# A local-attention and channel-mixing kernel on one core: the whole table that orders its steps is replaced

## The chip, the cores and the metric

The kernel runs on one core of a Trainium2 chip. The metric is the time of one execution on the device in microseconds (us); lower is better. Before the change three runs gave 621.28, 622.59 and 622.96 us, median 622.59 us.

## What is computed

The reference, cut to what matters (4 batches, 8 heads, 768 positions, 64 values a head):

```python
k_sum = k.reshape(B, H, nb, 32, D).max(axis=3)          # block maxima, 24 blocks
v_sum = v.reshape(B, H, nb, 32, D).mean(axis=3)         # block means
scores_l = scale * q @ k^T   where |i - j| < 16, else -1e9
scores_s = scale * q @ k_sum^T + log(32)
a = softmax(concat(scores_l, scores_s))                 # local window and block summaries
x = (a @ concat(v, v_sum)) laid out as [batch, 768, 512]
u = x + (x^T @ U @ V)^T                                 # U, V of rank 32, over the positions
out = u + relu(u @ w_ch1) @ w_ch2                       # 512 -> 2048 -> 512
```

## The kernel before the change

Everything is held in two parts (a high one and a rest) so that the products keep 32-bit accuracy; a product is therefore three matmuls. The bulk of the work is TensorE's (PE): for batch 0 the rows of `up` (L1015) and `down_rows` (L1037), for batches 1 to 3 the seven products of `up_phase` (L1300, inside `product`) and then `down_phase` (L1396) or, in batch 3, `second_phase` (L1498). All else is small steps round it: each batch's attention is done while PE works on the batch before it, and the weights are scaled, summed, stored to memory, fetched again and split as they are needed.

The order in which these steps are issued is a table of words, the string `PLAN` (L67 on). It has 481 pieces between slashes. After each piece of PE's main work the kernel runs the words of the next piece:

```python
def go():
    for word in next(plan).split():
        name = word.rstrip("0123456789.")
        words_of[name](*map(int, filter(None, word[len(name) :].split("."))))
```

The schedule is manual: every engine carries out its instructions in the order in which the words issue them, so a word's place fixes its place on PE, on the vector engine (DVE), the scalar engine (ACT), GpSimd (POOL) and on the queue of SyncE (SP), which issues all transfers one after the other. A transfer's issue waits on SP until its source is written, and everything behind it waits with it.

The first piece, up to the first slash, is the start-up: batch 0's attention (words with a leading dot), before PE's main work can begin. Its words load k, q and v of a head (`.lk`, `.lq`, `.lv`; L310, L324, L345), reduce block maxima (`.K`, L418), make scores (`.S`, L474), exponentials (`.E`), transposes, block means of v by a matmul (`.M`, L399), the value summaries (`.B`, `.D`, L437), values (`.V`, L599), the division by the sum (`.N`, L629), the mixing over positions (`.I`, L642, and what follows), and now and then four matmuls on zeros (`.w4`, L1139).

For a head h of batches 1 to 3 (written b.h) the words are, in the order of its data: scores `S` (PE L451), exponentials `E` (DVE L499, ACT L509), `T` (the weights are transposed in 32x32 squares, DVE L529), `s` (the squares go to memory, SP L534), `f` (four transfers bring them back transposed, SP L542), `P` (the values, PE L613) and `N` (the division, DVE L627 to L629, which writes `x`). The squares have one buffer. Then, for a pair of heads, `M` mixes over the positions (PE L642). For two of the four channel groups `x` is also transposed on the way through memory: `R` (DVE L554), `r` (SP L558, `rows<-place`), `g` (four transfers, SP L567, `place<-rows`), after which L692 on PE and L695 on DVE add the mixing to the rows. Other words met below are `w` (sums of weights, DVE L874 to L878), `y` (the low part of a gate, DVE L1374, 1.78 us in a row below), `O` (the operands of the seven products, among them DVE L743 and L757), `F` (a weight fetched, SP L929), `G` (parts of the down weights stored, SP L990, `halfA<-parts`), `Us`, `U` and `D` (SP L894, L883 to L885, L890), `v` (SP L338 and L339).

Of the kernel before, what the change touches and what calls it, by code (L numbers as in the profile page):

```python
# [73 lines left out]
    .S6 .Xl .C4 .la0 .S4 .K5 .Qs .E14.0 .Bd2 .Dp1 .E8.1 .V5 .E13.0 l1.0.0 .Kp5 .V4 .E8.2 .N0 .S5
    .E12.2 .E8.0 .V3 .V2 .E11.1 .E13.1 .E12.0 .M1 .lr .E9.0 .E12.1 .E11.2 .T12 .E13.2 .E11.0
    .E9.1 .T8 .T15 .Mo1 .Z0 .C12 .C15 .Dp6 .E10.2 .E10.1 .la1 .Qf .E10.0 .N1 .N2 .T13 .lb0 .T14
    .I0 .Y0.0 .T11 .E9.2 .Bd6 .Dd5 .T9 .Io0 .C11 .Bp4 .Bp7 .C13 .la2 .C8 .Y0.1 .Dp4 .V12 .lb1
    .C9 .V11 .V13 .Y0.2 .J0 .lb2 .V8 .N6 .la4 .Bp5 .T10 a1.0.0 .la3 .V9 .C14 .V14 .Jo0 .C10 q1.0
    .V10 .Dp7 .N4 k1.0 .G0.0 .V15 .G0.1 .lb3 .N5 .Z1 .N7 .Go0.0 a1.0.0 .G1.1 .Go0.1 .I2 .G1.0
    .Y1.0 .Io2 .J2 .z0 .w4 .Y1.1 .Jo2 .G0.2 .W0 .G0.3 .Y1.2 .Go0.2 l1.0.1 .Go0.3 .Z2 .G1.2  # L80
    .Go1.1 .Go1.2 a1.0.0 t2 W0.5 .G1.3 a1.0.0 .Go1.0 t2 .Go1.3 .U0.0 .W1 a1.0.0 / / / t2 c0.4 t2
    t2 a1.0.0 K1.0 .lb4 t2 c0.3 t3 a1.0.0 a1.0.1 w0.0 c1.2 / l1.1.0 w0.1 / x1.1 t3 x0.2 t3 v1.1
    D1 Ka1.0 v1.0 / c1.3 k1.1 S1.0.1 / E1.0.1.0 E1.0.1.1 W0.6 E1.0.1.2 S1.0.0 t3 a1.0.1 t4
    E1.0.0.1 t3 c0.5 E1.0.0.0 D0 K1.1 t5 a1.0.1 E1.0.0.2 a1.0.1 t3 Ka1.1 x0.3 w1.0 / T1.0 x1.2
    q1.1 k1.2 K1.2 / / c1.4 S1.1.0 a1.0.1 t4 / E1.1.0.2 W1.5 U0 S1.1.1 E1.1.0.0 a1.1.0 E1.1.0.1
    W1.6 s1.0 Ka1.2 q1.2 U1 w1.1 E1.1.1.2 E1.1.1.0 t4 a1.0.1 D2 E1.1.1.1 t4 k1.3 Us0 t4 t4 t5 t5
    Us1 f1.0 / c1.5 U4 a1.0.1 a1.0.1 x1.3 / D3 x0.4 a1.0.1 c0.6 / W0.7 t6 S1.2.0 t5 Ba1.1.1 U3
    T1.1 W0.8 E1.2.0.1 Ba1.0.0 E1.2.0.0 a1.1.0 E1.2.0.2 / t5 s1.1 t5 / q1.3 x0.5 W1.7 t6 x1.4
    a1.1.0 D4 S1.2.1 W0.9 Ba1.0.1 E1.2.1.1 K1.3 f1.1 E1.2.1.2 / E1.2.1.0 t6 / t6 c0.7 c0.8 P1.0
    Ba1.1.0 t6 / c1.6 W1.8 N1.0 T1.2 w2.0 t7 Ka1.3 t8 k1.4 / S1.3.0 / s1.2 E1.3.0.2 E1.3.0.0  # L90
    S1.3.1 t6 E1.3.0.1 q1.4 c1.7 P1.1 w2.1 k1.5 x1.5 E1.3.1.0 E1.3.1.1 t7 v1.2 E1.3.1.2 N1.1
    K1.4 x0.6 t7 T1.3 Ka1.4 / Ba1.2.1 / t7 v1.3 c1.8 q1.5 t7 w3.0 t7 / S1.4.0 Ba1.2.0 x1.6 U5
    f1.2 D5 E1.4.0.2 W1.9 R1.0 c0.9 t8 K1.5 x0.7 E1.4.0.0 w3.1 l1.1.1 t8 / Ba1.3.1 W0.10 / /
    E1.4.0.1 W0.11 S1.4.1 Ba1.3.0 E1.4.1.0 E1.4.1.2 E1.4.1.1 a1.1.0 t8 P1.2 t9 s1.3 t9 N1.2 t8
    t8 / / x1.7 T1.4 W1.10 x0.8 q1.6 Ka1.5 c0.10 U6 / a1.1.1 S1.5.0 t10 / f1.3 a1.1.0 E1.5.0.2
    S1.5.1 D7 W1.11 D6 E1.5.0.1 c1.9 t9 t10 E1.5.0.0 t9 t9 c0.11 k1.6 a1.1.1 E1.5.1.1 c1.11 t10
    U7 t11 t9 r1.0 / s1.4 a1.1.0 W0.12 E1.5.1.0 a1.1.1 t10 x1.8 / a1.1.0 g1.0 a1.1.1 E1.5.1.2
# [1567 lines left out]
```

## Time and profile before

| what | us |
|---|---|
| median of three runs (621.28 to 622.96) | 622.59 |
| the profiled execution's own time | 626.52 |
| its span, from the first to the last instruction | 624.3 |
| first matmul of the main work | 50.25 |
| busy: PE, weight loads of PE | 610.4, 557.9 |
| busy: DVE, ACT, POOL | 446.5, 350.9, 345.6 |

The profile shows one execution. "PE" is the matmuls and "PEld" PE's loading of the stationary operand, which overlaps them. A matmul's busy time ends where the profile models its end, so two matmuls in a row overlap in the record. Each row of an engine gives the time that the engine sat idle before it and, after an arrow, what ended that idleness. The chain of waits is followed back from the last instruction: each piece is an engine or a transfer on which the next piece waited.

### The profile page before, as it was taken

How to read it: one execution, taken by the hardware profiler on the slowest of the kernel's cores; microseconds unless marked ns; L12 is line 12 of the kernel's file. 1: busy time of each engine (PE TensorE's matmuls, PEld its weight loads, DVE VectorE, ACT ScalarE, POOL GpSimd, SP SyncE). 2: the span in 40 equal slices, each digit the busy share in tenths (PEclk: the TensorE clock that was granted, in tenths of full speed). 3: DMA queues.
4: the chain of work that ended last, by engine and by line, in shares of the span. 5: the costliest groups of instructions: out<-in, count | busy, mean ns of one | idle time of the engine just before them, and what ended most of it. 6: DMA issues, size and time to landing. Idle time of an engine off the chain costs nothing.

```text
span 624.3 us, 14694 instructions
## 1 busy us (share of the span) xinstructions
PE 610.4 (98%) x5376; PEld 557.9 (89%) x5376; DVE 446.5 (72%) x1139; ACT 350.9 (56%) x794; POOL 345.6 (55%) x393
## 2 busy tenths in 40 slices
...
GB/s 222 230 323 246 285 313 258 288 291 325 295 197 281 226 239 262 241 301 300 262 305 181 210 266 203 198 256 237 253 242 311 220 133 168 149 191 203 145 119 126
DMA packets 97559, 148.30 MB, mean 238 GB/s; under 512 B 9680, under 2 KB 67920, under 8 KB 97488
## 3 DMA queue, kind: packets, MB, share of 16 engines
...
q14 instruction: 29, 0.24, 0.1%
...
## 4 chain that ended last, share of the span: by engine, by line
PE 81%; DMA 12%; SPq 3%; DVE 1%; issue 1%; ACT 1%; POOL 1%; DVEq 0%; ACTq 0%
PE ps_h L1300 25%; PE acc L1396 17%; PE ps_h L1015 10%; PE acc L1037 10%; PE accx L1498 4%; PE accy L1498 3%; PE accz L1498 3%; DMA place<-in_k 2%; PE ps_x L613 2%; DMA dsum<-tmp 2%; PE ps_s L474 2%; PE ps_s L451 2%; DMA there<-squares 2%; SPq L542 1%; DMA whole<-up 1%; DMA place<-in_v 1%
## 5 line engine op out<-in xcount | busy, mean ns | idle before, releaser
L967 POOL TENSOR_TENSOR parts<-whole,parts 128x512 fp32r<-128x512 f32 (+1 forms) x128 | 159.3, 1258 | 77.3 <-ACT parts L963 72.9
L1300 PE MATMUL ps_h<-place,parts 128*128 128x384 f32 x1008 | 179.5, 336 | 0.7 <-DVE x L629 0.7
L1300 PEld LDWEIGHTS ps_h<-place,parts 128*128 128x128 f32 x1008 | 174.3, 188 | 3.0 <-PE ps_h L1300 1.0
L1396 PE MATMUL acc<-gh,parts 128*128 128x256 f32 (+1 forms) x512 | 133.6, 341 | 0.0
L1396 PEld LDWEIGHTS acc<-gh,parts 128*128 128x128 f32 x512 | 88.6, 189 | 12.3 <-issue 1.4
L963 ACT CAST parts<-whole 128x512 fp32r<-128x512 f32 (+1 forms) x144 | 80.8, 581 | 11.9 <-issue 4.6
L1396 PE MATMUL acc<-gl,parts 128*128 128x512 f32 (+1 forms) x256 | 86.5, 338 | 0.0
L1015 PE MATMUL ps_h<-place 128*128 128x384 f32 x384 | 73.9, 341 | 0.4 <-DVE x L695 0.3
L509 ACT ACTIVATE e<-e,neg 128x120 f32<-128x120 f32 x144 | 52.0, 390 | 33.4 <-DVE neg L499 32.3
L1015 PEld LDWEIGHTS ps_h<-place 128*128 128x128 f32 x384 | 67.2, 188 | 3.1 <-DVE x L695 0.7
L1037 PE MATMUL acc<-place,gh 128*128 128x512 f32 x192 | 66.5, 400 | 0.0
L1369 ACT ACTIVATE gh<-place 128x768 fp32r<-128x768 f32 x32 | 27.1, 846 | 62.2 <-PE acc L1396 62.2
L264 POOL TENSOR_SCALAR val<-place 128x512 f32<-128x512 f32 (+1 forms) x33 | 54.1, 1642 | 9.4 <-ACT place L244 4.4
L289 POOL TENSOR_TENSOR place<-val,place 128x512 fp32r<-128x512 f32 x29 | 37.6, 1301 | 29.7 <-ACT place L288 25.2
L1374 DVE SCALAR_TENSOR_TENSOR gl<-place,gh 128x768 fp32r<-128x768 f32 x32 | 38.3, 1196 | 20.3 <-ACT gh L1369 20.2
L1396 PEld LDWEIGHTS acc<-gl,parts 128*128 128x128 f32 x256 | 48.5, 189 | 4.5 <-DVE gl L1374 0.2
L743 POOL TENSOR_TENSOR place<-tmp,place 128x384 fp32r<-128x384 f32 x24 | 27.8, 1163 | 41.0 <-ACT place L739 34.2
L1037 PEld LDWEIGHTS acc<-place,gh 128*128 128x128 f32 x192 | 36.1, 188 | 7.4 <-ACT gh L1027 0.2
L499 DVE CUSTOM_DVE_ANT_0 e<-ps_s,mask_sb 128x120 f32<-128x120 f32 x144 | 35.1, 276 | 6.2 <-PE ps_s L451 4.1
L1027 ACT ACTIVATE gh<-ps_h 128x384 fp32r<-128x384 f32 x32 | 15.7, 489 | 41.0 <-PE ps_h L1015 40.9
L1037 PE MATMUL acc<-place,gl 128*128 128x512 f32 x96 | 37.7, 393 | 0.0
L1329 DVE TENSOR_TENSOR place<-place,ps_h 128x384 f32<-128x384 f32 x24 | 13.3, 554 | 28.7 <-PE ps_h L1300 28.6
...
## 6 DMA issues: line engine op xcount, KB each, us to landing
...
there<-squares SPq DMA_DIRECT2D x24, 384.0 KB, 4.8
at<-there SPq DMA_DIRECT2D x96, 96.0 KB, 3.4
whole<-up SPq DMA_DIRECT2D x24, 384.0 KB, 3.9
...
```

Source lines behind the costliest of these rows:

```text
L264: nc.gpsimd.tensor_scalar(f32(bits), f32(hi), 0.0, None, ALU.mult)
L289: engine.tensor_tensor(lo, val, f32(hi), ALU.subtract)
L499: nc.vector.tensor_tensor_reduce(out=e[:, u, :], in0=ps[:, i * KC : (i + 1) * KC], in1=mask_sb[:, m, :], scale=-SCALE, scalar=BIG, op0=ALU ...
L509: nc.scalar.activation(e[:, u, :], e[:, u, :], AF.Exp, bias=st.neg[h][:, u : u + 1], scale=-1.0,)
L963: nc.scalar.copy(hi, whole)
L967: (nc.vector if key[0] == "second" else nc.gpsimd).tensor_tensor(lo, whole, f32(hi), ALU.subtract)
L1015: nc.tensor.matmul(ps[:, :NH], w_split[0, f][:, c % 2, part_w, c // 2], ut[c], start=(n == 0), stop=(n == 3 * NC - 1),)
L1037: nc.tensor.matmul(acc[t], gt[:, sl], w_split[1, f][:, part_w], start=(first and j == 0), stop=(last and j == 2),)
L1300: nc.tensor.matmul(ps, a[:, sa, i], b[i][:, sb], start=(first and n == 0), stop=(n == 5), skip_group_check=not first,)
L1374: nc.vector.scalar_tensor_tensor(gl, h, 0.0, f32(gh), ALU.max, ALU.subtract)
L1396: nc.tensor.matmul(place, w[:, part_w, c * P : (c + 1) * P], gt[:, q0:q1], start=(f == 0 and i == 0 and j == 0), stop=(f == NF - 1 and j = ...
L1498: nc.tensor.matmul(ps, w[j][:, sa, c * P : (c + 1) * P], gate[sb], start=fresh and q == 0 and j == 0 and k == 0, stop=q == 3 and j == 1 an ...
```

## The change

The string `PLAN` is replaced by another with the same words: 1882 words in 481 pieces, each as often as before. No other line differs; what the words do is untouched. Nearly every line of the table differs, so two lines of each stand for it:

```diff
 PLAN = """
-    .lu .li .X .w4 .z1 .w4 .lk0 .lk3 .K0 .Xt0 .Kd0 .lq0 .lm .lq3 .lk2 .K3 .S0 .Kd3 .S3 .m .K2
-    .Kp2 .E0.2 .w4 .lq2 .E0.1 .lk1 .F .w4 .lq1 .E1.0 .E7.0 .E6.2 .E1.1 .lv0 .S2 .lv1 .E0.0 .E1.2
...
+    .lu .lq2 .lk0 .K0 .lk2 .lq0 .w4 .X .w4 .Kd0 .w4 .lq3 .K2 .lk3 .lm .S0 .Kp2 .K3 .S2 .Kd3 .m
+    .lk1 .S3 .E4.1 .E7.0 .li .K1 .E5.0 .E5.2 .E1.0 .E5.1 .lq1 .E1.2 .lv0 .E6.1 .E7.2 .lv1 .Xt0
...
```

Three places where the order of instructions moves follow, each as the lists of the two kernels have it: the line of the code, the operation, output and input tiles with their buffer numbers, and the shape.

**SP's queue where batch 1 sends the rows of its channel groups 2 and 3 through memory.** Before, the second `rows` transfer (`rows_2888`, word r1.3) stands behind the four fetches of the first (`place_2881`, word g1.2):

```order
L929 DMA whole_2763<-up0_104 128x1024
L558 DMA rows_2810<-place_2723 128x768
L894 DMA up5_109<-place_2218 128x512
L894 DMA up5_109<-place_2219 128x512
L929 DMA whole_2861<-up0_104 128x768
L567 DMA place_2881<-rows_2810 32x4x192 x4
L558 DMA rows_2888<-place_2830 128x768
L310 DMA kt_2890<-in_k 128x3x192
L929 DMA whole_2892<-up1_105 128x1024
L567 DMA place_2903<-rows_2888 32x4x192 x4
```

With the change the first `rows` transfer is `rows_2728`, the second `rows_2860`:

```order
L558 DMA rows_2728<-place_2643 128x768
L542 DMA at_2752<-there_2678 32x4x192 x4
L929 DMA whole_2759<-up0_104 128x1024
L894 DMA up5_109<-place_2209 128x512
L894 DMA up5_109<-place_2210 128x512
L890 DMA down_112<-val_2260 128x512
L567 DMA place_2831<-rows_2728 32x4x192 x4
L890 DMA down_112<-val_2631 128x512
L558 DMA rows_2860<-place_2836 128x768
L324 DMA qz0_84<-in_q0 64x384
L324 DMA qz0_84<-in_q1 64x384
L567 DMA place_2895<-rows_2860 32x4x192 x4
```

The first `rows` transfer has moved ahead of a head's fetch (L542, the last of batch 1) and stands further from its own fetches; a k load and a weight fetch no longer stand between the second `rows` transfer and its fetches, two q loads do.

**DVE's order where batch 2's last two heads are divided by their sums** (words N2.6 and N2.7: L627 to L629, the tiles `sum`). Before, both divisions follow one another behind an operand step and a gate (`gl_4821`):

```order
L984 TENSOR_TENSOR tmp_4813<-whole_4590,tmp_4806 128x256
L985 TENSOR_TENSOR tmp_4813<-whole_4590 128x256
L743 TENSOR_TENSOR place_4619<-x_3716,place_4619 128x384
L757 TENSOR_TENSOR tmp_4874<-x_3716 128x384
L1374 SCALAR_TENSOR_TENSOR gl_4821<-place_3772,gh_4820 128x768
L627 TENSOR_SCALAR sum_4888<-ps_x_4713 128x6
L628 RECIPROCAL sum_4888<-sum_4888 128x6
L629 TENSOR_TENSOR x_3716<-ps_x_4713,sum_4888 128x6x64
L627 TENSOR_SCALAR sum_4898<-ps_x_4848 128x6
L628 RECIPROCAL sum_4898<-sum_4898 128x6
L629 TENSOR_TENSOR x_3716<-ps_x_4848,sum_4898 128x6x64
L554 STREAM_TRANSPOSE place_4903<-x_3716 128x768
```

With the change:

```order
L984 TENSOR_TENSOR tmp_4836<-whole_4641,tmp_4676 128x256
L985 TENSOR_TENSOR tmp_4836<-whole_4641 128x256
L695 TENSOR_TENSOR x_3780<-ps_u_4839,place_4582 128x3x128
L627 TENSOR_SCALAR sum_4868<-ps_x_4843 128x6
L628 RECIPROCAL sum_4868<-sum_4868 128x6
L629 TENSOR_TENSOR x_3780<-ps_x_4843,sum_4868 128x6x64
L1374 SCALAR_TENSOR_TENSOR gl_4889<-place_3770,gh_4888 128x768
L757 TENSOR_TENSOR tmp_4903<-tmp_4730,x_3780 128x384
L433 COPY kt_4595<-km_4688 64x4x12 x4
L984 TENSOR_TENSOR tmp_4921<-whole_4690,tmp_4783 128x256
L985 TENSOR_TENSOR tmp_4921<-whole_4690 128x256
L554 STREAM_TRANSPOSE place_4951<-x_3780 128x768
```

The last division (`sum_4868`) now stands ahead of the gate (`gl_4889`) and of the operand step; the one of the head before it (`sum_4779`) stands ten rows above the first row shown. The transpose L554 has five rows of other work between the division and itself.

**SP's queue where head 4 of batch 1 is fetched** (word f1.4: `at<-there`, L542). Before, the squares were sent as `there_2001` ten rows above it:

```order
L894 DMA up3_107<-place_1709 128x512
L894 DMA up3_107<-place_1710 128x512
L542 DMA at_2204<-there_2001 32x4x192 x4
L883 DMA up1_105<-val_977 128x512
L883 DMA up5_109<-val_1930 128x512
L558 DMA rows_2248<-place_2118 128x768
```

With the change the squares (`there_2159`) are sent nineteen rows above it:

```order
L338 DMA vt_2332<-in_v 96x390
L339 DMA vt_2332<-in_v 96x390
L534 DMA there_2339<-squares_2220 128x768
L883 DMA up4_108<-val_1713 128x512
L883 DMA up5_109<-val_1947 128x512
L885 DMA up5_109<-val_2074 128x2x128
L890 DMA down_112<-val_1948 128x512
L542 DMA at_2396<-there_2159 32x4x192 x4
L802 DMA place_2449<-in_w2 128x1024
```

The fetch has moved down the queue, behind the sending of head 5's squares (`there_2339`), the rows of channel group 1 and two heads' loads of v; in the table it now stands in the same piece as the values of its head (P1.4).

## Rows read from the trace of the kernel before

**Rows 1.** The page: busy time, share of the span and instructions of each engine; the group of the seven products' matmuls (busy time, mean ns of one, idle time before them).

```profile
PE 610.4 (98%) x5376; PEld 557.9 (89%) x5376; DVE 446.5 (72%) x1139; ACT 350.9 (56%) x794; POOL 345.6 (55%) x393
...
L1300 PE MATMUL ps_h<-place,parts 128*128 128x384 f32 x1008 | 179.5, 336 | 0.7 <-DVE x L629 0.7
```

**Rows 2.** The chain of waits, in order of time: start, length (us), what.

```profile
25.46 7.87 DMA place<-in_v
...
50.25 4.30 PE ps_h L1015 x24
54.55 1.62 PE acc L1037 x7
...
504.08 56.16 PE ps_h L1300 x324
```

**Rows 3.** All waits of PE in the span: line, what was waited for, us in total, times, the longest (lines left out are of the start, none over 1.0 us).

```profile
PE ps_s L474 <- DMA x<-in_q: 3.5, 2, 2.8
PE ps_n L399 <- DMA place<-in_v: 1.2, 2, 0.8
...
PE ps_m L642 <- DVE x L629: 0.8, 2, 0.6
PE ps_h L1300 <- DVE x L629: 0.7, 1, 0.7
...
PE ps_x L613 <- DMA whole<-up: 0.4, 1, 0.4
PE ps_x L613 <- DMA at<-there: 0.4, 1, 0.4
PE ps_h L1015 <- DVE x L695: 0.3, 1, 0.3
PE ps_u L692 <- DVE x L695: 0.3, 1, 0.3
...
```

**Rows 4.** SP's queue from 183 to 198 us: start, us, the issue, and how many in a row (times are those of issuing, not of the transfer).

```profile
183.77 0.38 SPq L558 DMA_DIRECT2D rows<-place  x1
...
190.22 2.47 SPq L567 DMA_DIRECT2D place<-rows  x4
192.73 0.43 SPq L558 DMA_DIRECT2D rows<-place  x1
...
195.59 1.74 SPq L567 DMA_DIRECT2D place<-rows  x4
```

**Rows 5.** The chain of waits at the same place: the transfers of the second `rows` and of its fetch.

```profile
192.73 2.85 DMA rows<-place
...
196.91 4.40 DMA place<-rows
```

**Rows 6.** DVE at the same place: start, us, line, operation, and in brackets the idle time before it and what ended it.

```profile
189.91 0.98 DVE L554 STREAM_TRANSPOSE place<-x 128x768 f32<-128x768 f32 x1
...
196.91 1.51 DVE L878 TENSOR_TENSOR place<-val,place 128x256 f32<-128x256 f32 x1
198.46 0.56 DVE L695 TENSOR_TENSOR x<-ps_u,place 128x384 f32<-128x384 f32 x1
...
201.49 0.56 DVE L695 TENSOR_TENSOR x<-ps_u,place 128x384 f32<-128x384 f32 x1 [1.55 <-DMA place<-rows]
```

**Rows 7.** DVE from 334 to 338 us, same columns.

```profile
334.49 0.56 DVE L757 TENSOR_TENSOR tmp<-x 128x384 f32<-128x384 f32 x1 [1.81 <-DMA dsum<-tmp]
334.96 1.78 DVE L1374 SCALAR_TENSOR_TENSOR gl<-place,gh 128x768 fp32r<-128x768 f32 x1
336.66 0.15 DVE L627 TENSOR_SCALAR sum<-ps_x 128x6 f32<-128x6 f32 x1
...
337.96 0.56 DVE L629 TENSOR_TENSOR x<-ps_x,sum 128x384 f32<-128x384 f32 x1
```

**Rows 8.** DVE from 266 to 269 us, same columns.

```profile
266.28 0.98 DVE L529 STREAM_TRANSPOSE squares<-e 128x768 f32<-128x768 f32 x1 [2.03 <-POOL parts L967]
...
268.71 0.56 DVE L629 TENSOR_TENSOR x<-ps_x,sum 128x384 f32<-128x384 f32 x1
```

**Rows 9.** The page's transfer issues: operation, count, size of one, median us from issue to landing.

```profile
there<-squares SPq DMA_DIRECT2D x24, 384.0 KB, 4.8
at<-there SPq DMA_DIRECT2D x96, 96.0 KB, 3.4
```

**Rows 10.** SP's queue: the sending and the fetch for head 7 of batch 3, and what stands between.

```profile
465.91 0.38 SPq L534 DMA_DIRECT2D there<-squares  x1
...
466.81 3.52 SPq L990 DMA_DIRECT2D halfA<-parts  x4
470.45 2.57 SPq L542 DMA_DIRECT2D at<-there  x4
```

**Rows 11.** SP's queue and PE: the fetch for head 4 of batch 1 and the matmuls that read it.

```profile
137.06 3.35 SPq L542 DMA_DIRECT2D at<-there  x4
...
160.04 0.89 PE L613 MATMUL ps_x<-vt,at 120*32 120x65 f32 x48
```

**Rows 12.** Stretches of the span: us, busy us of PE, PEld, DVE, ACT and POOL with the count of instructions, PE's granted clock, busy share of the transfer engines, GB/s moved.

```profile
20.00:22.00 2.00, 1.88 (x78) 1.54 (x66) 0.75 (x3) 0.87 (x4) 0.60 (x2) 1.00 0.65 166
22.00:24.00 2.00, 1.49 (x34) 1.11 (x36) 1.57 (x5) 1.92 (x6) 1.74 (x6) 1.00 0.73 194
...
500.00:550.00 50.00, 50.00 (x290) 49.55 (x289) 23.20 (x39) 32.24 (x71) 34.13 (x31) 1.00 0.46 144
```

More of the change, by code (lines that the diff above doesn't have):

```diff
@@ L74 @@
[L74 to L97, printed above, removed]
@@ new lines @@
+    .V9 .Y1.0 .N5 .N4 .Y1.1 .G0.1 .w4 .I2 .Go0.1 l1.0.1 .Io2 .G0.0 .Go0.0 .J2 .G1.0 .Jo2 .lb2
+    .G1.1 .G0.3 .G0.2 .Y1.2 .G1.3 .la3 k1.0 .la4 .W0 .G1.2 .Go0.3 .Go0.2 k1.1 .Z2 t2 .Go1.0
+    .Go1.2 .Go1.1 a1.0.0 U0 .Go1.3 .U0.0 .W1 / K1.0 a1.0.1 a1.0.0 t2 w0.0 / a1.0.0 c1.2 / t2
+    a1.0.0 t2 t2 c0.3 t2 .lb3 / a1.0.1 a1.0.0 .z0 w0.1 t3 Ka1.0 a1.0.0 / S1.0.1 t3 x1.1 x0.2 /
+    c0.4 W0.5 v1.0 t4 / S1.0.0 E1.0.1.0 c0.5 .lb4 .z1 a1.0.1 D1 l1.1.0 W0.6 E1.0.1.2 c1.3
+    E1.0.1.1 t3 q1.1 a1.1.0 t3 E1.0.0.0 t3 a1.0.1 k1.2 E1.0.0.2 K1.1 E1.0.0.1 t3 q1.2 W1.5 t5 /
@@ new lines @@
+    E1.3.0.2 s1.2 E1.3.0.1 t7 D3 W1.7 E1.3.0.0 x1.5 S1.3.1 E1.3.1.0 t7 l1.1.1 E1.3.1.2 v1.3 W0.9
+    P1.1 Ba1.2.0 Ba1.2.1 E1.3.1.1 N1.1 W1.9 t7 Ba1.3.1 c1.8 k1.5 / w2.1 W0.10 K1.4 t7 Ka1.4 t7
+    c1.7 t7 c0.9 T1.3 U2 R1.0 t8 x1.6 / / a1.1.1 S1.4.0 E1.4.0.2 f1.2 E1.4.0.0 t8 K1.5 c1.9
+    a1.1.1 W1.10 E1.4.0.1 w3.0 t8 x0.7 / / t8 t8 / w3.1 S1.4.1 t8 U7 t9 q1.5 s1.3 D5 / r1.0
+    Ba1.3.0 / E1.4.1.2 t9 P1.2 U6 E1.4.1.0 x1.7 U5 Ka1.5 E1.4.1.1 c0.10 t9 t9 / N1.2 W0.11 /
+    S1.5.0 T1.4 x0.8 t10 a1.1.1 c0.11 E1.5.0.2 a1.1.0 E1.5.0.1 f1.3 t9 k1.6 g1.0 E1.5.0.0 /
```

190 lines of the change are left out of this document (101 added, 89 removed).

## Prediction

> **What bounds the kernel now.** I read the busy times first: PE is busy for 610.4 of 624.3 us [rows 1]. A busy PE need not be a PE at its peak, so I took a stretch in which it waits for nothing. The chain of waits stays on PE for 324 matmuls from 504.08 us, 56.16 us or 173 ns each [rows 2], and in 500 to 550 us PE's loads were busy for 49.55 of 50 us at full granted clock, with DVE at 23.20 and POOL at 34.13 [rows 12]. There a matmul starts as fast as its stationary operand can be loaded, and no order of the other engines' work makes that faster. An order can win only what PE waits for: the start, up to the first matmul of the main work at 50.25 us [rows 2], and the waits after it. Those are few: 0.8, 0.7, 0.4, 0.4, 0.3 and 0.3 us, 2.9 us in seven waits [rows 3].
>
> A shown wait is smaller than its delay. A matmul's record lasts 336 ns on average [rows 1] where one starts each 173 ns, so the record covers 0.16 us of the time after the next should have begun. I count shown time plus 0.16 us for each wait: 2.9 + 7 x 0.16 = 4.0 us after 50.25 us. That is the most that the order can win there.
>
> The Trainium skill, "Perfetto Trace Analysis", section Identifying the Most-Contended Engine, judges TensorE's headroom by the busy share of weight loads, not by that of matmuls. By that rule 624.3 - 557.9 = 66 us would be open to a better order, not 4 plus the start. The rows speak against it here: loads fill 99% of the wait-free stretch at one matmul each 173 ns, but one of L1037 takes 231 ns [rows 2], so that the same load fills some 74% of it with PE just as busy. I keep to the waits.
>
> **The change, place by place.** No word is added or removed, so the engines' work is the same, and the sum has terms only for waits that go or come. The gains:
>
> *A, batch 1's rows, 199 to 202 us: -0.9.* PE waits twice, 0.3 us each, on L695 [rows 3]. The second L695 sat idle for its fetch until 201.49 [rows 6]. The transpose that makes those rows was over at 190.89 (189.91 + 0.98) [rows 6], but they were sent at 192.73, when SP had issued the four fetches of the group before (190.22 to 192.69) [rows 4]; then 2.85 us to memory and 4.40 us back [rows 5]. The first L695 started at 198.46, behind L878, which ran 1.51 us from 196.91 [rows 6]. In the new order the first group's rows are sent ahead of a fetch and stand further from their own fetches, so SP should be past these by 190.9; the 1.8 us so won cover the 1.55 us of idleness. L877 and L878 now come behind three L695. Both waits go: 0.6 + 2 x 0.16 = 0.9. Bounds: 0 and -0.9.
>
> *B, batch 2's last divisions, 337 to 339 us: -1.1.* The mixing L642 waits twice, 0.8 us in all, on L629 [rows 3]. The two divisions stood behind an L757, which waited 1.81 us for a buffer until 334.49, and a gate of 1.78 us, and ran from 336.66 to 338.52 [rows 7]. Now N2.7 stands ahead of gate and operand step, N2.6 ten rows higher, and 32 matmuls of L1396 lie between N2.7's place and the mixing instead of 9, 5.5 us instead of 2.1. 0.8 + 0.32 = 1.1. Bounds: 0 and -1.1.
>
> *C, 269 us: -0.9.* One matmul of L1300 waits 0.7 us on L629 [rows 3] (the division N2.1, over at 269.27), which stood behind a transpose that had waited 2.03 us and began at 266.28 [rows 8]. The new order has the division ahead of that transpose. 0.7 + 0.16 = 0.9. Bounds: 0 and -0.9.
>
> *D, the values of head 2.3: -0.6.* They wait 0.4 us for their fetch [rows 3]. Between the fetch's place and theirs lay 2.0 us of PE's matmuls; now 5.8. 0.4 + 0.16. Bounds: 0 and -0.6.
>
> Together -3.5. Against them stand the places where the new order leaves less room.
>
> *E, the values of head 3.7: +0.5.* They wait 0.4 us, by the name of a weight fetch; their own fetch was issued last, at 470.45, behind four stores that took SP 3.52 us [rows 10]. These stores now follow the fetch, and four fetches of rows leave the queue ahead of the sending, which should come some 2.4 us sooner; the fetch must still let the sent squares land (4.8 us, [rows 9]; 470.45 - 465.91 = 4.5 before [rows 10]). But the values' own place is 2.8 us of PE's work nearer to the sending of head 3.6, which frees the one buffer of squares. 2.8 - 2.4 = 0.4, about 0.5. Bounds: -0.6, the wait gone, and +2, nothing won on SP.
>
> *F, the fetch of head 1.4: +0.5.* In the table of before 37 matmuls of L1015 at 179 ns, 36 of L1037 at 231 ns [rows 2] and a few others, 16.5 us, lay between the fetch and the values. Now nothing does. SP runs ahead of the table: the values began at 160.04, so the fetch's place was at 143.5, and SP reached it at 137.06 [rows 11], 6.4 us ahead. Issuing took 3.35 us there [rows 11] and landing takes a median 3.4 [rows 9], together 6.75. With the same lead the values wait 0.35 + 0.16 = 0.5. Bounds: 0, and 6.9 with no lead.
>
> *Other fetches nearer to their values: +0.6.* Four more lose room: 2.2 from 4.9 to 1.9 us, 2.7 from 2.8 to 1.4, 3.5 from 13.9 to 3.0, 3.6 from 4.6 to 1.9. Head 2.3 with 2.0 waited 0.4 [rows 3]; head 1.1 had 1.1 without a wait. I take one such wait of 0.4 + 0.16. Bounds: 0 and 2.2, all four.
>
> *The start: -0.4.* PE waits 3.5 us there for q, 1.2 for v [rows 3]. The last v is on the chain from 25.46 to 33.33 us [rows 2], behind nearly all of batch 0's loads, so the transfers decide. Their engines were at 0.65 and 0.73 in 20 to 24 us [rows 12]: 2 x 0.35 + 2 x 0.27 = 1.2 us of transfer time lost, while SP issued six small q loads in a row. The new order deals q and k out in turn; I take half, -0.6, and +0.2 because the mask comes later and the first exponentials with it. Bounds: -1.2, the dip filled, and +1.0, a dip elsewhere.
>
> **Sum.** -3.5 + 0.5 + 0.5 + 0.6 - 0.4 = **-2.3 us**. The profiled execution (626.52 us, 2.2 us more than its span) lies 3.9 us above the median of the three runs; it would become 624.2, its span 622.0. From the median, 622.59 - 2.3 = **620.3 us**.
>
> **Rivals.**
>
> *Waits only move, about 622.3.* DVE is busy 72% of the span [rows 1] and was late by 0.3 to 0.7 us at most of the places named; whatever is put ahead of something delays something else, and DVE's sum stays. For it: every word has moved, and I priced those places where I could see less room. Against it: the gates and sums that lose their places have some us before PE reads them. If A to D are half made up (-1.8) and E, F and the others stay (+1.6), the sum is -0.2 with a start unchanged.
>
> *A larger gain, about 617.9.* SP leads enough that E, F and the others cost nothing, and the transfer dip is filled: -3.5 - 1.2 = -4.7. For it: SP had 6.4 us of lead at F. Against it: the transfer engines are near 1 in the first half of the start, and a dip may come elsewhere.
>
> *Slower, by one late fetch, about 625.0.* At F the fetch shares its piece with its values, so all depends on SP's lead L. The wait is 6.75 - L + 0.16. The other terms are -2.8; the kernel becomes slower by over 1.87 us where -2.8 + 6.9 - L passes 1.87, for L under 2.2 us. With L = 1.7 the sum is +2.4. For it: 3.35 us for four issues [rows 11], where four of the rows' fetches took 1.74 [rows 4], is itself a queue that stalls, and head 1.5's sending and four stores now stand just ahead. Against it: that sending's squares are made ten us of PE's work before. The Trainium skill, "DMA: Bandwidth & Descriptors", section Rules for kernel authors, asks that a transfer be issued early and waited for late so that its fixed cost is hidden; F does the opposite, and by that rule this rival would be the likely one. The row of before, with SP 6.4 us ahead, speaks for a cost of 0.5.
>
> **Numbers.** A measurement of this kernel can tell about 0.3%, 1.87 us, from no change. The forecast has 0.45; its own spread, about 1.2 us either way, lies some three quarters beyond -1.87, which gives faster 0.33 and same 0.12. Waits only move: 0.24, same. Larger gain: 0.17, faster. Late fetch: 0.14, slower. Together faster 0.50, same 0.36, slower 0.14. The low end is all of 4.0 us of waits and 1.2 us of the start, -5.2: 617.4, say 617.2. The high end takes in waits that only move and the lighter part of the late fetch, +1.2: 623.8. Left out are most of the late fetch (0.10) and as much again on both sides.
>
> **What would show it.** PE's waits after the first L1015 should no longer name L695 in batch 1, nor L629 before L642 in batch 2 or before L1300; their sum should be under 2 us instead of 2.9. L642 near 337 us should start within 0.2 us of the end of the matmul before it. The values of head 1.4, near 160 us, should wait under 0.6 us, with the fetch's issue at least 6 us ahead of them. The first L1015 should start near 49.9 us, and the last matmul of PE 2.3 us sooner than before. It is wrong if waits of another name add up to 3 us or more, if the values of 1.4 wait over 2 us, or if the first L1015 comes after 51 us or before 48.5.

## The result: slower, by 0.7 to 1.2%

| | before | changed | ratio, 95% interval |
|---|---|---|---|
| first comparison, 4 runs each | 622.78 us (621.28 to 623.59) | 630.20 us (628.52 to 631.09) | 1.0119 (1.0090 to 1.0148) |
| second comparison (after_again below), 35 and 12 runs | 625.52 us (620.99 to 632.09) | 629.88 us (627.08 to 635.16) | 1.0070 (1.0041 to 1.0098) |

Forecast were 620.3 us and a range of 617.2 to 623.8. The runs of one kernel scatter more than the first three of before showed, so most of what follows is read from the traces, and each comparison has its interval. Three slow executions (632.09 and 629.16 us of before, 1516.27 us of newstart) stand in the medians and ranges and not in the ratios.

The changed kernel's profiled execution took 629.91 us, its span 628.1 us. Its page, first the busy times, then the group of the seven products:

```profile
PE 611.0 (97%) x5376; PEld 558.5 (89%) x5376; DVE 445.4 (71%) x1139; ACT 349.9 (56%) x794; POOL 344.9 (55%) x393
...
L1300 PE MATMUL ps_h<-place,parts 128*128 128x384 f32 x1008 | 180.2, 336 | 0.2 <-DVE o L1542 0.2
```

The work is as before ([rows 1]); more idle time stands between. All waits of PE in it, to be held against [rows 3] (us in total, times, the longest):

```profile
PE ps_s L474 <- DMA x<-in_q: 2.8, 1, 2.8
PE ps_x L613 <- DVE neg L499: 2.2, 1, 2.2
PE ps_x L613 <- DMA at<-there: 2.0, 3, 1.2
PE ps_s L474 <- POOL place L433: 1.5, 1, 1.5
PE ps_u L684 <- DVE t_st L670: 1.0, 1, 1.0
...
PE ps_u L692 <- DVE x L695: 0.6, 1, 0.6
PE ps_h L1300 <- DVE o L1542: 0.2, 1, 0.2
```

The waits of places A to E are gone: no L1015 on L695, no L642 or L1300 on L629 in the main work, and the values of heads 2.3 and 3.7 (P2.3, P3.7) are not among those that wait for a fetch. F did not cost anything either. But others have come: 2.2 + 2.0 + 0.6 + 0.2 = 5.0 us in six waits after the start, where there were 2.9 in seven, and a wait of 1.0 us (L684) at the end of the start. Three places carry nearly all of it.

**Place G, the values of head 2.5, 312.8 us: 2.2 us, in all five profiles that have this order** (changed, after_again, after_filler, after_fetch, oldstart; two of the expectations below call it head 2.6). PE at that place (start, us, line, in brackets the idle time before and what ended it):

```profile
310.00 0.60 PE L660 MATMUL ps_r<-t,rep_sb 128*128 128x256 f32 x2
312.77 0.89 PE L613 MATMUL ps_x<-vt,at 120*32 120x65 f32 x48 [2.17 <-DVE neg L499]
```

and DVE, same columns:

```profile
307.62 0.27 DVE L499 CUSTOM_DVE_ANT_0 e<-ps_s,mask_sb 128x120 f32<-128x120 f32 x1
307.82 0.08 DVE L499 DVE_READ_ACCUMULATOR2_ANT neg<- 128x1 f32 x1
310.63 0.42 DVE L981 TENSOR_TENSOR tmp<-whole 128x256 f32<-128x256 f32 x1 [2.74 <-PE ps_r L660]
...
311.88 0.42 DVE L982 TENSOR_TENSOR tmp<-tmp,whole 128x256 f32<-128x256 f32 x1
312.23 0.28 DVE L499 CUSTOM_DVE_ANT_0 e<-ps_s,mask_sb 128x120 f32<-128x120 f32 x1
...
312.43 0.28 DVE L499 CUSTOM_DVE_ANT_0 e<-ps_s,mask_sb 128x120 f32<-128x120 f32 x1
```

Two sums of down weights (words d5.0 and d3.0, L981 and L982) stand ahead of the last two exponentials of head 2.7. The first sum writes into one of eight buffers shared by name (`val`), and the buffer whose turn it is holds the operand of L660, which PE reaches at 310.00. So DVE idles for 2.74 us with two exponentials behind it. These free a bank of scores (the memory that PE writes has its banks in one rotation, for scores and values alike) that PE's next matmuls, the values of head 2.5, need; they start at 312.77, 0.06 us after the last read-out. PE waits for DVE, which had waited for PE. The Trainium skill, "TensorE: Matmul & The Clock Gate", section "Architectural detail: the array is 16× 32×32, not 1× 128×128", calls DVE's queue strictly first in, first out; the trace agrees: in the 2.74 us the exponentials don't overtake.

In three of the five profiles this wait costs more than it shows: behind it PE's granted clock fell to the lower of its two levels (0.50 in the rows, 1.2 GHz instead of 2.4). The same stretch, first in after_again, where PE had stood idle from 310.13 to 312.30, then in the first profile of the changed kernel, where the clock did not fall (columns as in [rows 12]):

```profile
314.00:316.00 2.00, 2.00 (x6) 1.52 (x6) 1.87 (x5) 0.27 (x2) 1.28 (x1) 0.51 0.41 106
314.00:316.00 2.00, 2.00 (x10) 1.62 (x9) 1.86 (x3) 0.74 (x2) 1.30 (x1) 1.00 0.25 62
```

Six matmuls start in 2 us instead of ten. The matmul that is 150 places behind the wait came after 15.23 us in the first profile and 15.19 in after_filler, both at full clock, and after 16.75, 16.76 and 16.65 us in after_again, after_fetch and oldstart: 1.5 us on top of the 2.2.

**Place H, three fetches of squares: 1.2, 0.5 and 0.3 us.** The largest, head 2.0. SP, then PE:

```profile
242.67 0.32 SPq L929 DMA_DIRECT2D whole<-up  x1
244.24 0.81 SPq L360 DMA_DIRECT2D stage<-in_vn  x2
245.10 1.85 SPq L542 DMA_DIRECT2D at<-there  x4
```
```profile
253.19 0.89 PE L613 MATMUL ps_x<-vt,at 120*32 120x65 f32 x48 [1.18 <-DMA at<-there]
```

SP stood still from 242.99 to 244.24, at a load (l2.1.1) whose buffer an addition on POOL had not yet given back, with the fetch behind it. Landing then took long, as the chain of waits has it:

```profile
246.52 6.43 DMA at<-there
```

The profile's page gives 3.5 us as the median of these fetches. For head 1.6, SP stood for 1.9 us (170.18 to 172.12) at a k load, L310, then issued l2.0.0, and the fetch at 174.33; for head 2.2 the four issues of the fetch alone took 4.11 us from 268.28.

**Place I, the end of the start.** The chain of waits from SP's queue to the first L1015, which [rows 2] has at 50.25:

```profile
37.75 6.93 DMA place<-in_w
...
44.70 0.69 ACT place L244
...
45.47 1.53 POOL val L264
...
47.02 0.69 DVE val L270
...
48.68 0.44 DVE t_st L670
...
49.16 0.44 PE ps_u L684
...
51.13 4.44 PE ps_h L1015 x24
```

A weight load is issued at 37.75, its step on DVE (Y1.1, L270) is late, and what stands behind that on DVE (Jo2, L670) makes PE wait. The weight loads were issued late because SP waited at another load:

```profile
28.52 0.43 SPq L802 DMA_DIRECT2D place<-in_w  x1
33.02 0.81 SPq L360 DMA_DIRECT2D place<-in_vn  x2
33.87 1.47 SPq L1150 DMA_DIRECT2D rep_sb<-in_rep  x1
```

For 4.1 us (28.95 to 33.02) nothing behind l1.0.0 could be issued: it writes where batch 0's v still had to be read by PE. The transfer engines show it (columns as in [rows 12], the last but one is their busy share):

```profile
20.00:24.00 4.00, 4.00 (x98) 3.82 (x89) 1.90 (x6) 2.19 (x8) 1.70 (x3) 0.84 1.04 270
28.00:37.00 9.00, 8.54 (x233) 7.30 (x229) 7.97 (x51) 7.58 (x25) 3.52 (x10) 1.00 0.65 183
```

In the first profile of before the same stretches have 0.69 and 1.00: the dip that the prediction wanted filled is filled, and a longer one has come behind it.

In the start PE's granted clock was also at its lower level (columns as in [rows 12]):

```profile
7.00:8.00 1.00, 0.00 (x0) 0.00 (x0) 0.88 (x6) 0.00 (x0) 0.00 (x0) 0.80 1.06 238
16.00:18.00 2.00, 2.00 (x20) 1.70 (x13) 1.50 (x15) 2.00 (x9) 0.00 (x0) 0.50 1.09 236
21.00:22.00 1.00, 1.00 (x43) 0.91 (x36) 0.00 (x0) 0.16 (x2) 0.00 (x0) 0.88 1.00 224
```

The 0.80, 0.50 and 0.88 say that it fell within the eighth microsecond and came back in the twenty-second; in the first profile of before it was 1.00 throughout the start. Three theories followed. Theory 1, the first suspicion: the start costs the time, by its lower clock. Theory 2: the new waits of places G and H cost it. Theory 3: the late weight loads of place I make the end of the start late.

### The profile page after: what moved, and what is told of

Its sections match the earlier page's. It is cut to its first block, busy times and chain, and to the rows that moved or that the text cites. A ratio compares the mean times of both kernels' runs of the same rounds, so it can differ in the third digit from the quotient of the medians.

```text
span 628.1 us, 14706 instructions
## 1 busy us (share of the span) xinstructions
PE 611.0 (97%) x5376; PEld 558.5 (89%) x5376; DVE 445.4 (71%) x1139; ACT 349.9 (56%) x794; POOL 344.9 (55%) x393
## 4 chain that ended last, share of the span: by engine, by line
PE 79%; DMA 10%; DVE 3%; POOL 3%; SPq 2%; issue 1%; ACT 1%; POOLq 0%; ACTq 0%; DVEq 0%
PE ps_h L1300 22%; PE acc L1396 18%; PE ps_h L1015 10%; PE acc L1037 9%; PE accx L1498 4%; PE ps_s L474 3%; PE ps_x L613 3%; PE accy L1498 3%; PE accz L1498 3%; DMA at<-there 2%; DMA place<-in_w 2%; PE ps_s L451 1%; POOL parts L967 1%; DMA whole<-down 1%; DMA down<-val 1%
## 5 line engine op out<-in xcount | busy, mean ns | idle before, releaser
L967 POOL TENSOR_TENSOR parts<-whole,parts 128x512 fp32r<-128x512 f32 (+1 forms) x128 | 161.7, 1279 | 104.8 <-ACT parts L963 95.7
L1300 PE MATMUL ps_h<-place,parts 128*128 128x384 f32 x1008 | 180.2, 336 | 0.2 <-DVE o L1542 0.2
L1300 PEld LDWEIGHTS ps_h<-place,parts 128*128 128x128 f32 x1008 | 174.2, 188 | 2.9 <-issue 0.6
L1015 PE MATMUL ps_h<-place 128*128 128x384 f32 x384 | 74.5, 342 | 0.0
L1015 PEld LDWEIGHTS ps_h<-place 128*128 128x128 f32 x384 | 66.8, 188 | 2.5 <-DVE place L715 0.3
L264 POOL TENSOR_SCALAR val<-place 128x512 f32<-128x512 f32 (+1 forms) x33 | 51.5, 1564 | 13.6 <-ACT place L244 9.4
L743 POOL TENSOR_TENSOR place<-tmp,place 128x384 fp32r<-128x384 f32 x24 | 26.2, 1104 | 19.7 <-ACT place L739 19.7
```

Source lines behind the costliest of these rows:

```text
L264: nc.gpsimd.tensor_scalar(f32(bits), f32(hi), 0.0, None, ALU.mult)
L967: (nc.vector if key[0] == "second" else nc.gpsimd).tensor_tensor(lo, whole, f32(hi), ALU.subtract)
L1015: nc.tensor.matmul(ps[:, :NH], w_split[0, f][:, c % 2, part_w, c // 2], ut[c], start=(n == 0), stop=(n == 3 * NC - 1),)
L1300: nc.tensor.matmul(ps, a[:, sa, i], b[i][:, sb], start=(first and n == 0), stop=(n == 5), skip_group_check=not first,)
```

## Experiments

The ratio is to runs of before on the same chip. "Start" is the first L1015, "main" the time from it to the start of PE's last matmul, both from the one profile of each kernel. A profile can lie off its kernel's median, 2 to 3 us below for newstart, after_both, both_y and both_early and 4.9 above for oldstart_both, so start and main say what happened in one execution and the ratio what the kernel costs.

| kernel | runs | median us | ratio (95%) | start | main |
|---|---|---|---|---|---|
| before (first profile) | | | | 50.09 | 570.38 |
| before_again | 10 | 624.69 | 1.0000 (0.9974 to 1.0025) | 48.80 | 570.26 |
| newstart | 12 | 626.99 | 1.0025 (1.0001 to 1.0049) | 49.12 | 569.82 |
| oldstart | 7 | 629.18 | 1.0064 (1.0038 to 1.0090) | 48.18 | 575.48 |
| changed (first profile) | | | | 50.96 | 572.05 |
| after_again | 12 | 629.88 | 1.0070 (1.0041 to 1.0098) | 50.50 | 573.56 |
| after_filler | 6 | 633.29 | 1.0125 (1.0086 to 1.0163) | 54.08 | 573.80 |
| after_e_first | 12 | 628.62 | 1.0050 (1.0023 to 1.0077) | 51.43 | 570.61 |
| after_fetch | 12 | 630.23 | 1.0062 (1.0033 to 1.0090) | 50.42 | 574.33 |
| after_both | 12 | 626.75 | 1.0018 (0.9988 to 1.0047) | 49.23 | 569.60 |
| both_y | 12 | 627.20 | 1.0047 (1.0020 to 1.0075) | 47.45 | 570.78 |
| both_early | 12 | 627.01 | 1.0046 (1.0020 to 1.0071) | 50.28 | 568.62 |
| both_early_y | 8 | 629.70 | 1.0080 (1.0047 to 1.0114) | 51.81 | 571.59 |
| both_l | 12 | 625.18 | 1.0011 (0.9989 to 1.0033) | 49.38 | 570.05 |
| before_gains | 12 | 627.34 | 1.0032 (1.0004 to 1.0061) | 52.24 | 569.27 |
| oldstart_both | 10 | 628.68 | 1.0080 (1.0051 to 1.0109) | 51.95 | 575.31 |

Main is PE's fixed work and its waits: taking off each profile's waits after the start, 0.16 us more for each (as the prediction counts them) and 1.5 us in the four profiles where the clock fell behind a wait (before_again, oldstart, after_again, after_fetch) leaves 565.8 to 567.0 us in all sixteen, where main itself runs from 568.6 to 575.5.

**before_again.** No edit.

> The kernel before, unchanged, for a second profile: its first profiled execution (626.52 us) lay 3.9 us above its median, while the changed kernel's profiled ones are like its median. If the first profile caught a poor execution, this one has a span near 620.5 us, and the place where 3.7 us are missing tells which waits of the first profile are not typical. If the first profile was typical, the span is again near 624.

The profile has a span of 622.9 us at a time of 624.68, which is the median here. The first profile was not a poor one: the three runs first shown were good ones. What differs from the first profile is the start, 1.3 us, not the main part, 0.1; and yet the waits are others:

```profile
PE ps_s L474 <- DMA x<-in_q: 3.0, 1, 3.0
PE ps_s L474 <- POOL place L433: 2.1, 2, 1.6
PE ps_x L613 <- DVE neg L499: 2.1, 1, 2.1
```

After the start PE waits 2.1 us on exponentials before the values of head 2.4, which did not wait in the first profile, and 0.3 us of place A is left; waits at B, C, D and E are not in the list. Behind the 2.1 us the clock fell here too, from 296.9 to 300.3 us, and the next 150 matmuls took 1.5 us longer than in the first profile. The same program, run again, had most of its waits elsewhere. newstart, whose later pieces are those of before, has A's first wait (0.3 us at 198.5), B (1.0) and C (0.6) again, and not D and E.

**newstart and oldstart.** The start-up words in the other kernel's order, before each kernel's own later pieces (a few words that only one of the two has in the start stay in theirs):

```diff
 newstart:
-    .lu .li .X .w4 .z1 .w4 .lk0 .lk3 .K0 .Xt0 .Kd0 .lq0 .lm .lq3 .lk2 .K3 .S0 ...
+    .lu .lq2 .lk0 .K0 .lk2 .lq0 .w4 .z1 .X .w4 .Kd0 .w4 .lq3 .K2 .lk3 .lm .S0 ...
 oldstart: the same the other way round, on the changed kernel
```

> The new order of the start-up piece alone (the words of the old piece in the order of the new), all later pieces as before. Theory 1 (the start is what costs: PE's granted clock falls to half about 7.8 us into the changed kernel and comes back at 21 us): slower than before by 4 us or more, the granted clock again at half in 8 to 20 us, the first L1015 later than 50.5 us. Theory 2 (the new waits after the start cost, above all 2.2 us before the values of head 2.6): slower by at most 1.5 us.

> The old order of the start-up piece, all later pieces as changed. Theory 1 (the start with its lower clock): within 2.5 us of before, no stretch of lower clock, the first L1015 near 50 us. Theory 2 (the new waits): slower than before by 4 us or more, with the 2.2 us wait before the values of head 2.6 still there.

The new start alone cost 0.25%, 1.6 us (0.1 to 3.1); the new later pieces alone 0.64%, 4.0 us (2.4 to 5.6), of which about 1.5 goes with the join of one kernel's start and the other's pieces (1.3 us of wait for POOL near 62 us, and 0.16), a wait that neither kernel has. Theory 2 holds for the larger part: the 2.2 us at place G are there in oldstart, with 1.5 for the clock behind them, and fetches cost 2.2. Against theory 1, newstart's clock was lower in 7.7 to 11.2 and 14.6 to 18.0 us and its first L1015 came at 49.12, not later than 50.5; oldstart had a lower stretch that was not expected, 8.4 to 11.8, and the first L1015 at 48.18. Where newstart's 1.6 us lie its profile doesn't show: it is of an execution 2.3 us below the median.

**after_filler.**

```diff
-    .lu .lq2 .lk0 .K0 .lk2 .lq0 .w4 .X .w4 .Kd0 .w4 .lq3
+    .lu .lq2 .lk0 .K0 .lk2 .lq0 .w4 .X .w4 .Kd0 .w4 .w4 .lq3
```

> The changed kernel with one more word of four matmuls on zeros behind the first three, in the idle time of PE before the first scores (5.4 to 8.2 us). If PE's idleness there is what lets the granted clock fall, it stays at 1.00 through the start, and theory 1 expects the time to fall by 3 us or more against the changed kernel (about 626 us); theory 2 expects under 1 us. If the clock falls in spite of it, something else of the order decides it.

Slower still, 1.0125, with a start of 54.08. The lower clock came later and for less time, from 14.8 to 18.2 and 28.4 to 31.8 us, instead of not at all, and none of the theories expected the loss. What made this start so late is not settled.

**after_again, after_e_first, after_fetch, after_both.**

```diff
 after_e_first:
-E2.7.1.1 E2.7.1.2 d5.0 Ds0 Ds4 / r2.1 / / d3.0 E2.7.0.1 h1.7 E2.7.0.2 p0 y1.7 J2.0 P2.5
+E2.7.1.1 E2.7.1.2 Ds0 Ds4 / r2.1 / / E2.7.0.1 h1.7 E2.7.0.2 d5.0 d3.0 p0 y1.7 J2.0 P2.5
 after_fetch:
-l2.1.1 ... f2.0    l2.0.0 ... f1.6    q2.6 f2.2
+... f2.0 l2.1.1    ... f1.6 l2.0.0    f2.2 q2.6
 after_both: both
```

> The changed kernel itself, on the same chip and in the same rounds as the three variants below, so that they can be compared with it. Theory 2 (new waits after the start cost about 4 us, the new start 1.5 to 2): some 1.0 to 1.2% over before, waits of PE again 2.2 us before the values of head 2.5 and about 2 us for fetches.

> The changed kernel with the two sums d5.0 and d3.0 behind the last two exponentials of head 2.7 instead of ahead of them. Theory 2: the sums wait on DVE for a buffer that a matmul L660 of PE gives back, PE's next matmuls (the values of head 2.5) wait for banks that the exponentials behind the sums give back; with the exponentials ahead the 2.2 us wait is gone, and the time falls by 1.5 to 2.3 us. Rival (the wait is for something else that comes no earlier, or other work takes its place): the time stays within 0.5 us.

> The changed kernel with three loads moved behind a fetch on SP's queue (l2.1.1 behind f2.0, l2.0.0 behind f1.6, q2.6 behind f2.2). Theory 2: the values of heads 2.0, 1.6 and 2.2 wait 1.2, 0.5 and 0.3 us because their fetches stand behind loads that wait; with the loads behind them these waits go, the time falls by 1.5 to 2.5 us. Rival (transfers are slow there, 5.3 us to landing instead of 3.4, whatever their order): at least half of these waits stays.

> Both edits. Theory 2: the gains add up, 3.5 to 4.5 us, and what is left over before is the start, some 2 us. Theory 1 (the start makes most of the difference): at least 4 us over before remain.

after_again lies 0.7% above before, under the 1.0 to 1.2 expected; place G has its 2.2 us again, but fetches cost only 1.0 us in two waits, and another 0.7 falls on the values of head 2.2.

With the exponentials ahead, place G is mended. DVE and PE of after_e_first:

```profile
309.16 0.27 DVE L499 CUSTOM_DVE_ANT_0 e<-ps_s,mask_sb 128x120 f32<-128x120 f32 x1
311.35 0.43 DVE L981 TENSOR_TENSOR tmp<-whole 128x256 f32<-128x256 f32 x1 [1.91 <-PE ps_r L660]
```
```profile
310.71 0.60 PE L660 MATMUL ps_r<-t,rep_sb 128*128 128x256 f32 x2
311.24 0.89 PE L613 MATMUL ps_x<-vt,at 120*32 120x65 f32 x48
```

The sum still waits for L660, as the theory of the shared buffer says, and PE does not wait there at all. Main falls from 572.05 and 573.56 to 570.61, by 1.4 and 2.9 us; 1.5 us of the larger step is the clock, which did not fall here. The median fell by 1.3 us, too little to tell two kernels with intervals of 0.3% apart; that the wait is gone, and why, is read from the trace.

With the loads behind the fetches the values of 2.0, 1.6 and 2.2 no longer wait, but in that profile other values do, 0.9 us in all, and PE waits 1.0 us on L1347; main did not fall (574.33), nor did the time by more than can be told. The waits of these three fetches went, as the theory says and the rival does not; the time that they should have given did not come. Both edits together gave 0.52% (1.0070 to 1.0018), 3.1 us between the medians, and main 569.60, and this is all that PE waits for from 49 us on:

```profile
PE ps_h L1300 <- ACT place L1347: 1.0, 1, 1.0
PE ps_u L692 <- DVE t_st L670: 0.4, 1, 0.4
PE ps_h L1015 <- DVE x L629: 0.4, 1, 0.4
PE ps_s L474 <- DVE x L695: 0.2, 1, 0.2
```

2.0 us instead of 5.0, and no lower clock after the start. With the new start, mending these two places takes back nearly the 3.5 to 4.5 us expected, and what is left, 0.18%, can't be told from no loss. How much of it each place gives can't be told from the times.

**both_y, both_early, both_early_y, both_l.** All on after_both, in the start:

```diff
 both_y:       -.Y1.1 .G0.1 ... .J2 .G1.0 .Jo2        +.G0.1 ... .J2 .G1.0 .Jo2 .Y1.1
 both_early:   the words up to .M1 in the order of before, the rest as changed
 both_early_y: both of these
 both_l:       -.M1 .C13 l1.0.0 .N2 ... .lb0 q1.0     +.M1 .C13 .N2 ... .lb0 l1.0.0 a1.0.0 q1.0
```

> The changed kernel with both earlier edits (sums behind the exponentials, loads behind the fetches) and one more: in the start-up, the second step of turning a weight (Y1.1, DVE, waits for a weight load) behind the step Jo2 (DVE L670) for which PE's L684 waits 1.0 us. Theory 3 (in the start the weight load comes late and what stands behind it on DVE makes PE wait): the 1.0 us wait is gone, the first L1015 comes 0.8 to 1.2 us sooner, at 48.2 to 49.8 us; the time lies at that of before within 0.3%. Rival (the start is bound by the lower clock and the loads before 25 us): another wait takes its place and the first L1015 stays where it was.

> Both earlier edits, and the start-up piece in the old order up to the block means M1 (word .M1), in the new order behind it. Theory 1 (the lower clock in 8 to 21 us, and the order of q, k and v loads behind it, cost the start its 1 to 2 us): granted clock near 1.00 there, first L1015 sooner than 49.5 us, time no more than before. Theory 3: the first L1015 stays within 0.7 us of that with the new order unless the weight load comes sooner too, because the loads behind M1 decide.

> Both earlier edits, the old order up to M1, and Y1.1 behind Jo2. If theories 1 and 3 both hold, the first L1015 is the earliest of these kernels (48 to 48.5 us) and the time is below that of before by 0.1 to 0.4%.

> Both earlier edits, and in the start-up the load l1.0.0 (SP L360), with the addition that reads it, behind three weight loads instead of right behind M1. In the changed kernel SP stood at this load from 28.95 to 33.02 us with the weight loads queued behind it. Theory 3: with it out of the way the weights are issued 2 to 4 us sooner, Y1.1 no longer waits, and the first L1015 comes about 1 us sooner, as with Y1.1 moved. Rival: the weight's place in memory is not free sooner, and nothing changes.

Moving Y1.1 takes L684's wait away, and the first L1015 came at 47.45, even sooner than expected; but 1.6 us come back among the first L1015, and the kernel is slower than before (1.0047), where 0.3% was expected at most:

```profile
PE ps_h L1015 <- DVE place L715: 1.6, 1, 1.6
```

The turned weight itself is needed there, so the step's place on DVE was not what cost the time. With l1.0.0 out of SP's way a weight load is issued at 28.86 us instead of 33.95 (after_both) and the next at 35.82 instead of 36.33; L684 does not wait, and the kernel is the one closest to before, 1.0011 (0.9989 to 1.0033). But its first L1015 came at 49.38, where after_both has 49.23: the start did not come 1 us sooner, as theory 3 expected. SP only stood at the next thing instead: from 29.29 to 32.98 us, before the four transfers of L1130. The old words up to M1 do not help (1.0046, start 50.28): the clock fell here too, against the expectation of theory 1, and the start is 1.05 us later than after_both's, more than the 0.7 of theory 3.

both_early_y bears on the clock. Its PE stood idle for 4.0 us before the first scores, longer than in any other, and its clock stayed at its higher level throughout:

```profile
8.00:12.00 4.00, 3.23 (x49) 2.74 (x49) 2.71 (x14) 0.18 (x1) 1.39 (x8) 1.00 0.75 195
12.00:16.00 4.00, 4.00 (x50) 3.73 (x51) 3.93 (x31) 3.23 (x11) 1.69 (x7) 1.00 1.03 231
16.00:20.00 4.00, 3.21 (x59) 2.35 (x57) 2.46 (x21) 3.96 (x14) 0.00 (x0) 1.00 1.04 253
20.00:24.00 4.00, 2.15 (x82) 1.82 (x82) 0.97 (x4) 1.90 (x7) 1.28 (x5) 1.00 0.77 152
```

Its first L1015 came at 51.81, where the earliest of all was expected, and the time is 1.0080. both_early, which differs from it by the place of Y1.1 alone, had the lower clock from 8.5 to 12.0 us and came at 50.28. The four profiles with the higher level all through the first 24 us (both of before, before_gains, this one) have it at 48.80 to 52.24, 50.7 on average; the twelve others, with a lower stretch somewhere in the start, at 47.45 to 54.08, 50.2 on average. So the starts with a lower clock were not later on the whole, and theory 1 has no support; with starts that scatter by 3 us, a loss of one microsecond would not be seen. What the new start's 1.6 us are stays open.

**before_gains.** The moves of places A to E alone, in the old order:

```diff
-g1.2 J1.2 r1.3 k2.1 F / ... w7.1 x1.15    -T2.3 S2.4 ... N2.1    -k2.6 p0 q2.6 E2.5.0.1 f2.3
+r1.3 g1.2 J1.2 k2.1 F / ... O1.1.1 w7.1   +N2.1 T2.3 S2.4 ...    +N2.2 f2.3 p1 / ... k2.6 p0 q2.6
-P2.6 ... P2.7 ... N2.6 / p1 O2.0.3 N2.7   -G8 G6 ... G7 f3.7
+P2.6 N2.6 ... P2.7 N2.7                   +f3.7 G8 G6 ... G7
```

> The kernel before with only the moves of places A to E of the prediction: r1.3 ahead of g1.2 and the sums w7.1 behind the first operands (A); N2.6 and N2.7 right behind the values of their heads (B); N2.1 ahead of the transpose T2.3 (C); f2.3 three pieces sooner (D); f3.7 ahead of the stores (E). The sum of the prediction for A to D was -3.5 us, and E by itself -0.6: if these gains are there to be had alone, the time falls by 2 to 4 us, and PE no longer waits at these places. If a wait that goes there is made up soon behind it, or the waits of the one profile were not those of most executions, it falls by less than 1 us.

Not faster: 1.0032 (1.0004 to 1.0061). The waits of A to E are gone, but PE waits at other places:

```profile
PE ps_h L1300 <- ACT place L1347: 0.8, 1, 0.8
PE ps_m L642 <- DVE x L629: 0.6, 1, 0.6
PE acc L1396 <- POOL parts L967: 0.6, 1, 0.6
```

Main is 569.27 against 570.38 and 570.26: 1.0 us, where the sum had 3.5 and 0.6 more. The 2.9 us of old waits after the start are gone, and these 2.0 us of new ones stand in their place. The start, whose words are those of before, came at 52.24 in this profile, 2 to 3 us later. Whether that is scatter or goes with this kernel, whose measured time is above that of before, isn't settled.

**oldstart_both.** The start of oldstart, the later pieces of after_both.

> The changed kernel with both edits after the start (sums behind exponentials, loads behind fetches) and the start-up words in the old order. If the new start costs 1 to 2 us and the new waits the rest, this lies within 0.3% of the kernel before; the join of the old start with the new pieces made PE wait 1.3 us for POOL near 62 us in the earlier run, which is to be taken off. If it is slower by more than 0.5%, something after the start that is in neither edit costs too.

1.0080: slower by more than 0.5%, also with the join's 1.5 us (0.24%) taken off. oldstart, from which it differs by the two edits alone, had 1.0064 (1.0038 to 1.0090): behind the old start the two edits won nothing that can be told. Its profile, of the slowest of its ten executions, has no wait at place G, but the join's wait for POOL again (1.3 us) and a fetch that comes 2.0 us late at 277 us, neither of which after_both had with the new start. By its expectation something after the start that is in neither edit costs too; what that is, is not shown, and this run doesn't price the start.

## Why the prediction was wrong

- **What bounds the kernel** was right: PE's work is unchanged, and the time went into PE's waits and the start.
- **A to D, -3.5, and E**: the waits of A to D went, each at its place, and that of E too, which was to grow by 0.5. The price of a wait was right as well: shown time plus 0.16 us accounts for main in all sixteen profiles to within 1.2 us, once the clock is counted. The step that failed is the sum: it took a removed wait as time won and set only +1.6 us against it for waits that come. Alone, those moves took all 2.9 us of waits away and 2.0 us of others came: 1.0 us of main and no measurable gain (before_gains). In the changed kernel 5.0 us came. And a second execution of the kernel before had most of the old waits somewhere else (before_again). A wait seen in one profile is partly that execution's; that the lateness behind it, of DVE and of SP's queue, remains and makes another matmul wait is how I read it, and no run separates it. Of A the mechanism also was off: `rows_2860` was sent at 192.80, not by 190.9, since its transpose had only just ended, and PE did not wait all the same.
- **F and the late fetch**: it cost nothing. SP issued the fetch at 152.98, 8.3 us ahead of the values at 161.27, where I had counted 6.4 and a wait of 0.5. The Trainium skill's rule to issue early ("DMA: Bandwidth & Descriptors", Rules for kernel authors) was kept all the same, by SP's lead of 8.3 us; a place in the table is not yet a time.
- **Other fetches, +0.6**: measured 2.0 us in three waits, 1.0 in two in after_again. The places were sought where the fetch stood near its values in the table. Two of the three (heads 2.0 and 1.6, with 6.7 and 3.1 us between) had room by that measure; ahead of them in the queue SP stood at a load whose buffer was not yet free, 1.25 us at l2.1.1 and 1.9 us at a k load.
- **The start, -0.4**: the new start alone measured +1.6 (0.1 to 3.1). The dip in the transfers before 25 us was filled as forecast; the dip elsewhere, which I had as the bound of +1.0, came in 28 to 37 us, with the stall of 4.1 us at l1.0.0. But filling that one too (0.90 instead of 0.65 in both_l) did not bring the first L1015 sooner. The step that failed here is that the transfers decide when the start ends; what costs the 1.6 us stays open.
- **What the sum lacked** was place G, 2.2 us in each profile of the unmended order and 3.7 with the lower clock that followed in three of five: a step on DVE whose buffer PE frees, ahead of steps that PE needs. Nothing in the trace of before shows it; in the new order it can be read (two sums between exponentials, L660 right ahead of the values), if one asks of every moved step which buffer it writes and who frees it.
- **The rivals.** "Waits only move" is what happened, at 0.24; I let it end at no change, and it ended 1.7 to 3.3 us worse in main (572.05 and 573.56 against 570.3), 1.5 of the 3.3 by the clock. (Its sum, -0.2 from 622.59, gives 622.4 and not the 622.3 written there.) The slower rival named another place, F, and the wrong one.

## What to carry to other kernels

When an order is changed everywhere, the waits of one profile say how much there is to win and not that it will be won: profile the old kernel twice before pricing its waits. For each moved step ask what it holds and what it needs: the buffer it writes and who frees it, and what stands behind it on its engine or queue. Here two sums ahead of two exponentials and loads ahead of fetches, waiting for buffers, gave back what the new order had won after its start, and one wait of PE could cost more than it shows, by the clock behind it; with the two mended the kernel was level with the old one again (1.0018, 0.9988 to 1.0047), and none tried was faster than it. Behind the old start the same two edits won nothing that could be told, so a mended wait has to be measured in the order that it is meant for.

## What the runs showed of the chip

- With the same start-up words the first L1015 came at 50.09 and 48.80 us in two executions of before and at 52.24 in one of before_gains, so some 3 us of scatter lie in the first 50 us alone; main, of the same later pieces, was 570.38, 570.26 and 569.82 (newstart).
- PE's granted clock fell to the lower of its two levels (0.50, 1.2 GHz) about 7.6 us into the changed kernel, when PE had been idle from 5.43 us, and rose at about 21 us; after 4.0 us of idleness in both_early_y, with the same words as both_early up to M1, it did not fall.
- After the start PE had seven waits of 2.0 to 2.2 us in these profiles. The clock fell behind four of them (before_again at 296.9 us; oldstart, after_again and after_fetch at 312 to 313) and not behind the other three (changed, after_filler, oldstart_both). Where it fell, the matmuls behind it lost 1.4 to 1.5 us.
